# Turning the head order of a fused attention-and-MLP training step so that four V heads stay on the chip, with the middle of the kernel rewritten by columns

## The chip, the core and the metric

One core of one Trainium2 chip. The metric is the device time of the whole program in microseconds; it is given as the median of several runs. Engines: TensorE (PE), VectorE (DVE), ScalarE (ACT), GpSimd (POOL) and SyncE (SP), which here does little but issue DMA transfers. Sixteen DMA engines move the data between the memory (HBM) and the on-chip buffer.

## What is computed

A decode step of a pre-layernorm transformer block (4 sequences, one token each, 32 attention heads over a cache of 4096 positions, model width 512, a gated MLP of width 1792) and its gradients with respect to the input, the whole K and V caches and all weights.

```python
def _A_ref(x, k_cache, v_cache, wq, wo):      # x [4,1,512], caches [4,32,4096,128] bf16
    q = (x @ wq) split into 32 heads of 128
    scores = einsum("bhqd,bhkd->bhqk", q, k_cache) * 128 ** -0.5
    p = softmax(scores)
    o = einsum("bhqk,bhkd->bhqd", p, v_cache)
    return o.reshape(4, 1, 4096) @ wo
def _B_ref(x, w1, w3, w2):
    return (silu(x @ w1) * (x @ w3)) @ w2
h = x + _A_ref(layernorm(x), k_cache, v_cache, wq, wo)
out = h + _B_ref(layernorm(h), w1, w3, w2)
# returned: out, and the vector-Jacobian product with grad_out for
# x, k_cache, v_cache, wq, wo, w1, w3, w2
```

The caches make up nearly all of the traffic: 128 pairs of sequence and head ("heads" below, number s = 4 x head + sequence), each with 1 MiB of K and 1 MiB of V, are read, and gradients of the same sizes are written. V is read twice, once in the forward part and once in the backward part.

## The kernel before

**Memory.** One on-chip tile, `arena`, is cut by hand into 23 slots of 4160 bf16 columns (`Slot`, L125). A slot holds one head of K or V, one transposed K, one product P x K (`PK`), a page of weights or an outgoing gradient. Slots are handed out in the order of the program text from a queue of free ones; the hardware then waits until the last user of that slot is through. The program order is written out by hand (`manual_schedule`): each engine executes its instructions in the order of the text, and all large transfers, loads and stores alike, are issued on SP's queue in that order. A few small ones go through POOL's queue.

**Forward loop** (L650 to L712). 64 rounds of two heads. For each head K is transposed (a quarter by PE and ACT, three quarters by DVE), the scores are formed, softmax runs over a chain of small steps (`sm_max` to `sm_P`), P x K is formed on DVE (`PK_mul`), and PE accumulates V^T x [PK, P] (`M_mm`): a 128 x 128 matrix M, kept for the gradient of q, and the attention output as its last column. `M_end` adds the sums of P x K (`kP`), copies M out and returns the slots of PK and V. `kP_flush` (L490) turns the k sums of 32 heads into columns; `O_cols` (L501) collects attention outputs. Towards the end `weights` (L628) loads wo in four pages and w1 and w3 in two halves each into slots as they become free.

**The end of the forward part** (L714 to L746). The last three heads' M alternate with `attn_page` (L510): the attention output times wo, rows of 512 columns on PE, eight heads to a page, added to the rows of x (`hrows`) by DVE in three additions. `woT` transposes wo in place, two heads to a unit, sixteen units in all; of these two are done here.

**The middle** (L843 to L969). First `while free: load_V2()` queues V heads for the backward part into all slots that are free: heads 0 to 6. Then: layernorm of h by rows of 4 partitions, with the results transposed and spread; two wo units; the gate product, four units of `w13T` (transposing w1 and w3 in place, 16 units in all), the up product; the activation and its gradient on DVE; the twelve other w13 units; the down product for the gradient (`dn_ps`, L906), column by column, 112 matmuls. Then the slots of w1 and w3 come free, one becomes `reps`, and two more V heads are queued (7 and 8). The layernorm's backward gives dhT; `rep_ps` and `dO_columns` (L768) multiply it by the first transposed wo page; `grad_V(0)` and `grad_V(1)` write the first two outer products on DVE and store them. `V_T(0, ...)` transposes V of head 0 by pairs of words, four groups, each four PE transposes and one ACT copy: two groups ahead of dhT, two behind `dO_columns`.

**The backward loop** (L1457 on). For heads 0 to 31 one by one, then in pairs: `front(s)` (L1230) transposes V and forms dP on PE; `more_V` (L1416) writes V gradients ahead of that; after four heads the group's dS is formed and `grad_K` writes K gradients. Side work is spread over the heads by `side` (L1449): the rest of wo's transposes and dO (`rest_of_dO`, L1163, in heads O0 = 2 to S0 = 21), the gradient of q (`dq_work`, L1005), and all small gradients (from S1 = 35). The free slots of this part are chosen by age.

Of the kernel before, what the change touches and what calls it, by code (L numbers as in the profile page):

```python
# [15 lines left out]
G = 2  # L16
# [7 lines left out]
OLD = 9  # L24


@with_exitstack
def kernel(
# [38 lines left out]
    GW = 8  # L67
# [19 lines left out]
    def bh_of(s):  # L87
        return s % B, s // B

# [72 lines left out]
    rows_t = pers.tile([32 + B, D], FP32, name="rows_t")  # L162
    xr, xhat = rows_t[0:B, :], rows_t[32:32 + B, :]
    nc.gpsimd.dma_start(out=xr, in_=x2)
    gr_s = Slot("gr")
# [7 lines left out]
    Ks, Vs, KTs, PKs = {}, {}, {}, {}  # L173

    def load_K(s):
        if s < NH:
            Ks[s] = Slot("Kn")
            nc.sync.dma_start(out=Ks[s].heads(), in_=cache_head(A_k_cache, s))
# [3 lines left out]
    def load_V(s):  # L182
        if s < NH and s >= nvl["n"]:
            nvl["n"] = s + 1
            Vs[s] = Slot("Vn")
            nc.sync.dma_start(out=Vs[s].heads(), in_=cache_head(A_v_cache, s))
# [16 lines left out]
    sel_f = fcon.tile([P, H], FP32, name="sel_f")  # L203
# [37 lines left out]
    hrows = xr  # L241
    kPT = pers.tile([P, NH], FP32, name="kPT")
# [83 lines left out]

    def M_of(s):
        return Ms[s // MC].f(MC * (Dh + 1)).rearrange("p (n c) -> p n c", c=Dh + 1)[:, s % MC, :]
# [37 lines left out]
    def q_stationaries(gi):  # L366
        W = fw.tile([P, G, 4, 32], BF16, name="W", tag="W", bufs=1)
        for hl in range(G):
            s = gi * G + hl
# [69 lines left out]
    def sm_P(gi):  # L439
# [5 lines left out]
        for q in range(4):  # L445
            r_ = slice(32 * q, 32 * (q + 1))
            nc.scalar.copy(out=P_all[r_, gi * G:(gi + 1) * G, :].rearrange("p g (c jj) -> p g c jj", c=4),  # L447
                           in_=v[r_, 0:G, :, :, q])

    def PK_pairs(s):  # L450
        PKs[s] = Slot("PK")
        PK = PKs[s].t[:].rearrange("p (j c) -> p j c", c=PKW)
        nc.gpsimd.tensor_copy(out=PK[:, :, Dh:PKW], in_=P_all[:, s, :, None].to_broadcast([P, SJ, 2]))  # L453
# [20 lines left out]
    def M_end(s):  # L474
# [13 lines left out]
        Vs.pop(s).give()  # L488

    def kP_flush(s):  # L490
        ks = Slot("kP_sb")
        kP_sb = ks.f(4 * Dh).rearrange("p (c d) -> p c d", c=4)
        nc.scalar.copy(out=kP_sb, in_=hold["kP"][:])
        kt_ps = psM.tile([P, PKW], FP32, tag="M", name="kt_ps")
        for c in range(4):
            nc.tensor.matmul(kt_ps[:, 0:H], lhsT=kP_sb[:, c, :], rhs=sel_f[:], start=(c == 0), stop=(c == 3))
        nc.scalar.copy(out=kPT[:, s - 31:s + 1], in_=kt_ps[:, 0:H])
# [3 lines left out]
    def O_cols(s0, s1):  # L501
        nc.vector.tensor_copy(out=OT_f[:, s0:s1], in_=Ms[s0 // MC].f(MC * (Dh + 1)).rearrange("p (n c) -> p n c", c=Dh + 1)[
            :, s0 % MC:s0 % MC + s1 - s0, Dh])
        nc.vector.tensor_copy(out=OT_bf[:, s0:s1], in_=OT_f[:, s0:s1])
# [5 lines left out]
    def attn_page(pg):  # L510
        last = pg == H // 8 - 1
        if pg == 0 or last:
            hold["at"] = psT.tile([P, 512], FP32, tag="tps", name="al_ps") if last else psX.tile([P, 512], FP32, tag="x", name="at_ps")
        at_ps = hold["at"]
        for k in range(8):
            c = 0 if last else k % 2
            nc.tensor.matmul(at_ps[32 * c:32 * c + B, :], lhsT=OT_bf[:, (8 * pg + k) * B:(8 * pg + k + 1) * B],
                             rhs=wo_page(8 * pg)[:, k].rearrange("p c n -> p (c n)"),
                             start=(k == 0 if last else pg == 0 and k < 2), stop=(k == 7 if last else pg == H // 8 - 2 and k >= 6),
                             tile_position=(0, 32 * c))  # L520
        if pg >= H // 8 - 2:
            for c in range(1 if last else 2):
                nc.vector.tensor_tensor(out=hrows, in0=hrows, in1=at_ps[32 * c:32 * c + B, :], op=ALU.add)
# [67 lines left out]
    def w13T(n, eng=None):  # L591
        for k in range(n):
            w13T_unit(*tunits.popleft(), eng[k % len(eng)])

    def w13T_unit(nm, i, k, eng):
        n = min(4, FC - k)
        v = mid_w[nm][i].b(2 * F).rearrange("p (c f) -> p c f", c=2)[:, :, k * P:(k + n) * P]
        pt = psT.tile([P, 2, 4, P], BF16, tag="tps", name="pt_w13")
# [3 lines left out]
        evac_copy(v.rearrange("p c (n k) -> p c n k", k=P), pt[:, :, 0:n, :], eng)  # L602
# [16 lines left out]
    tunits = deque((nm, i, k) for nm in ("w1", "w3") for i in range(2) for k in range(0, FC, 4))  # L619

# [29 lines left out]
    for gi in range(NGI):  # L650
# [23 lines left out]
        if has1:  # L674
            M_end(m1)
            load_V(m1 + VQ)
            if m1 % 32 == 31:
                kP_flush(m1)
# [50 lines left out]
    attn_page(0)  # L729
# [3 lines left out]
    attn_page(1)  # L733
    woT(2, "sv")
# [3 lines left out]
    O_cols(NH - MC, NH)  # L738
    attn_page(2)
    attn_page(3)  # L740
    kP_flush(NH - 1)
    weights(NGI)
    assert not pending
    c1b.close()
# [14 lines left out]
    rstd_h = pers2.tile([B, 1], FP32, name="rstd_h")  # L759
    mv_h = pers2.tile([B, nc.vector.BN_AGGR_DIM], FP32, name="mv_h")  # L760
# [29 lines left out]
    V2s, VTs = {}, {}  # L790
# [43 lines left out]
    nv = {"next": 0}  # L834
# [8 lines left out]
    with ExitStack() as cm:  # L843
# [3 lines left out]
        psT = cm.enter_context(tc.tile_pool(name="psTm2", bufs=4, space=bass.MemoryType.PSUM))  # L847
        while free:
            load_V2()

        pt = psA.tile([P, DC, B], FP32, tag="rT", name="pt_hT")
        for c in range(DC):
            nc.tensor.transpose(pt[:, c, :], hrows[0:B, c * P:(c + 1) * P], ident_f[0:B, 0:B])
        stats = small.tile([B, 1, nc.vector.BN_STATS_DIM], FP32, tag="ln_stats", name="ln_stats")
        nc.vector.bn_stats(out=stats[:, 0, :], in_=hrows)
        mv = mv_h
        nc.vector.bn_aggr(out=mv[:], in_=stats[:])
        nc.vector.tensor_scalar(out=rstd_h[:], in0=mv[:, 1:2], scalar1=eps, scalar2=None, op0=ALU.add)
        nc.scalar.sqrt(rstd_h[:], rstd_h[:])
        nc.scalar.activation(out=warm[:], in_=warm[:], func=AF.Exp)  # L860
        woT(2, "s")
        rdiag = mid.tile([B, 2 * B], FP32, name="rdiag")
        nc.vector.tensor_scalar(out=rdiag[:, 0:B], in0=ident_f[0:B, 0:B], scalar1=mv[:, 0:1], scalar2=None, op0=ALU.mult)
        nc.vector.reciprocal(out=rstd_h[:], in_=rstd_h[:])
        nc.vector.tensor_scalar(out=rdiag[:, B:2 * B], in0=ident_f[0:B, 0:B], scalar1=rstd_h[:], scalar2=None, op0=ALU.mult)
        rb_ps = psA.tile([P, 2 * B], FP32, tag="rT", name="rb_ps")
        nc.tensor.matmul(rb_ps[:], lhsT=ones_f[0:B, :], rhs=rdiag[:], start=True, stop=True)
        rb = mid.tile([P, 2 * B], FP32, name="rb")
        nc.vector.tensor_copy(out=rb[:], in_=rb_ps[:])
        hhatT = mid.tile([P, DC, B], BF16, name="hhatT")  # L870
        hhatT_f = mid.tile([P, DC, B], FP32, name="hhatT_f")
        nc.vector.tensor_tensor(out=hhatT_f[:], in0=pt[:], in1=rb[:, None, 0:B].to_broadcast([P, DC, B]), op=ALU.subtract)
        nc.vector.tensor_tensor(out=hhatT[:], in0=hhatT_f[:], in1=rb[:, None, B:2 * B].to_broadcast([P, DC, B]), op=ALU.mult)
        nc.vector.tensor_tensor(out=hhatT_f[:], in0=hhatT_f[:], in1=rb[:, None, B:2 * B].to_broadcast([P, DC, B]), op=ALU.mult)
        w1, w3 = mid_w["w1"], mid_w["w3"]
        gu_ps = psC.tile([P, 2, FC, B], FP32, tag="cols", name="gu_ps")
        for wi, wt in enumerate((w1, w3)):
# [4 lines left out]
            if wi == 0:  # L882
                w13T(4, "sv")
# [663 lines left out]
```

## Time and profile before

| | |
|---|---|
| median of 3 runs | 1688.55 us (1687.66 to 1689.11) |
| span of the profiled execution | 1686.6 us |
| PE, DVE, ACT, POOL busy | 1260.6, 1233.9, 960.9, 379.6 us |
| DMA | 707.21 MB, mean 419 GB/s |
| chain that ended last, by engine | DMA 35%, DVE 7%, ACT 5%, PE 5% |
| mean granted TensorE clock | 0.855 |

The profile lists for one execution when each engine was busy and what it waited for. The chain of waits follows the work that ended last back to the start. The tables by stretches give for a window of time the busy microseconds of each engine with the number of instructions, the granted TensorE clock (1.00 is full speed), the mean busy share of the DMA engines and the rate. The lines for SP show when a transfer was issued, not when it landed; the time to landing is listed with the issues by line. Two rows of that list:

```profile
arena<-in_A_v_cache_dram SPq DMA_DIRECT2D x160, 1024.0 KB, 15.6
out_dram<-arena SPq DMA_DIRECT2D x72, 1024.0 KB, 19.8
```

The columns are what is moved, the issuing queue, the number of transfers, the size of each and the median time from issue to landing in microseconds: a transfer stands behind several others.

### The profile page before, as it was taken

How to read it: one execution, taken by the hardware profiler on the slowest of the kernel's cores; microseconds unless marked ns; L12 is line 12 of the kernel's file. 1: busy time of each engine (PE TensorE's matmuls, PEld its weight loads, DVE VectorE, ACT ScalarE, POOL GpSimd, SP SyncE). 2: the span in 40 equal slices, each digit the busy share in tenths (PEclk: the TensorE clock that was granted, in tenths of full speed). 3: DMA queues.
4: the chain of work that ended last, by engine and by line, in shares of the span. 5: the costliest groups of instructions: out<-in, count | busy, mean ns of one | idle time of the engine just before them, and what ended most of it. 6: DMA issues, size and time to landing. Idle time of an engine off the chain costs nothing.

```text
span 1686.6 us, 33967 instructions
## 1 busy us (share of the span) xinstructions
PE 1260.6 (75%) x14188; PEld 924.3 (55%) x14188; DVE 1233.9 (73%) x1198; ACT 960.9 (57%) x1492; POOL 379.6 (23%) x663
## 2 busy tenths in 40 slices
PE   5989888888888888878878666667766677776660
PEld 4777777677667766745555544544434444444440
DVE  5999899989998997667766476576565656555673
ACT  3455454445445454677666556666655676666650
POOL 1221222222232222234541131111120101011020
PEclk9999999999999999799899778777678676567775
DMA  9999999999999999999999999999999999999996
GB/s 400 424 424 424 425 423 425 424 424 421 418 423 411 424 411 397 398 410 426 425 426 428 429 429 429 431 430 429 429 430 430 429 429 431 430 429 431 430 429 259
DMA packets 80986, 707.21 MB, mean 419 GB/s; under 512 B 8748, under 2 KB 12984, under 8 KB 15296
## 3 DMA queue, kind: packets, MB, share of 16 engines
q1 hardware_dynamic: 80416, 704.94, 99.2%
q8 instruction: 112, 1.84, 0.4%
q14 instruction: 42, 0.34, 0.0%
q0 software_dynamic: 416, 0.10, 0.0%
HBM read 422.59 MB, written 282.34 MB: 418 GB/s over the span
## 4 chain that ended last, share of the span: by engine, by line
DMA 35%; DVE 7%; ACT 5%; PE 5%; issue 3%; DVEq 0%; SPq 0%; POOL 0%; ACTq 0%
DMA out_dram<-arena 34%; DVE arena L1400 7%; ACT arena L799 5%; PE pt_tps L798 1%; PE dq_ps L1007 1%; PE dP_ps L1245 1%; DMA arena<-in_A_v_cache_dram 1%; PE pt_wo L610 0%; DVEq L1542 0%; PE rep_ps L1186 0%; DVE dPr L1342 0%; ACT dPr L1221 0%; PE dOT_ps L773 0%; PE dPT_ps L1228 0%; PE c_ps L784 0%
## 5 line engine op out<-in xcount | busy, mean ns | idle before, releaser
L799 ACT COPY arena<-pt_tps 128x1024 bf16<-128x1024 bf16 x512 | 491.7, 1023 | 249.0 <-PE pt_tps L798 247.3
L798 PE MATMUL pt_tps<-ident_f,arena 128*128 128x128 f32 x2048 | 410.7, 356 | 202.9 <-DMA arena<-in_A_v_cache_dram 125.6
L798 PEld LDWEIGHTS pt_tps<-ident_f,arena 128*128 128x128 f32 x2048 | 304.1, 182 | 349.3 <-issue 191.6
L1400 DVE TENSOR_TENSOR arena<-arena 128x8192 bf16<-128x8192 bf16 x48 | 212.5, 4427 | 197.9 <-DMA out_dram<-arena 192.5
L457 DVE TENSOR_TENSOR arena<-arena 128x4096 bf16<-128x4096 bf16 x128 | 292.4, 2285 | 24.0 <-POOL arena L453 24.0
L472 PE MATMUL M_ps<-arena 128*128 128x130 bf16 x4096 | 286.9, 223 | 30.0 <-DMA arena<-in_A_v_cache_dram 29.2
L472 PEld LDWEIGHTS <-arena 128*128 128x128 bf16 x4096 | 254.6, 99 | 49.6 <-DMA arena<-in_A_v_cache_dram 42.5
L1400 DVE TENSOR_TENSOR arena<-dS,arena 128x8192 bf16<-128x8192 bf16 x48 | 212.3, 4424 | 67.6 <-DMA out_dram<-arena 67.6
L364 DVE STREAM_TRANSPOSE arena<-arena 128x512 f32<-128x512 f32 (+1 forms) x321 | 250.6, 797 | 0.0
L359 ACT COPY arena<-pt_tps 128x1024 bf16<-128x1024 bf16 x128 | 129.4, 1012 | 180.4 <-PE pt_tps L358 149.6
L1397 POOL COPY arena<-arena 128x128 bf16<-128x128 bf16 x48 | 43.7, 912 | 432.7 <-ACT arena L1374 200.0
L370 POOL TENSOR_TENSOR W<-qrep,wmask 128x128 bf16<-128x128 bf16 x128 | 120.8, 944 | 85.4 <-PE S_ps L390 70.6
L453 POOL COPY arena<-P_all 128x64 bf16<-128x64 bf16 x128 | 32.7, 256 | 412.5 <-ACT P_all L447 409.5
L1308 POOL COPY arena<-arena 64x4 bf16<-64x4 bf16 x96 | 68.8, 717 | 136.3 <-PE dP_ps L1328 108.6
L1328 PE MATMUL dP_ps<-arena 128*32 128x512 bf16 x768 | 84.4, 471 | 8.4 <-ACT arena L799 8.3
L813 DVE TENSOR_TENSOR arena<-dS,arena 128x4096 bf16<-128x4096 bf16 x32 | 73.1, 2291 | 21.8 <-DMA out_dram<-arena 21.5
L447 ACT COPY P_all<-pt_P 32x64 bf16<-32x64 bf16 x256 | 52.1, 203 | 54.1 <-PE pt_P L443 51.8
L358 PE MATMUL pt_tps<-ident_b,arena 128*128 128x128 bf16 x1024 | 80.8, 224 | 0.0
L482 PE MATMUL kP_ps<-arena,onesw 128*32 128x512 bf16 x1024 | 79.4, 387 | 0.0
L813 DVE TENSOR_TENSOR arena<-P,arena 128x4096 bf16<-128x4096 bf16 x29 | 66.3, 2291 | 17.7 <-DMA out_dram<-arena 17.5
L422 ACT ACTIVATE E<-S_ps,nm 128x256 f32<-128x256 f32 x64 | 30.4, 474 | 82.7 <-DVE nm L419 82.6
L991 PE MATMUL gps<-arena 4*128 4x512 bf16 x110 | 47.3, 452 | 39.0 <-ACT arena L985 39.0
(246 smaller groups left out, 1494.7 us busy)
## 6 DMA issues: line engine op xcount, KB each, us to landing
out_dram<-arena SPq DMA_DIRECT2D x96, 2048.0 KB, 27.4
arena<-in_A_v_cache_dram SPq DMA_DIRECT2D x160, 1024.0 KB, 15.6
arena<-in_A_k_cache_dram SPq DMA_DIRECT2D x128, 1024.0 KB, 15.4
arena<-in_A_v_cache_dram SPq DMA_DIRECT2D x48, 2048.0 KB, 31.7
out_dram<-arena SPq DMA_DIRECT2D x72, 1024.0 KB, 19.8
arena<-in_A_wq_dram SPq DMA_DIRECT2D x8, 1024.0 KB, 14.3
arena<-in_B_w_dram SPq DMA_DIRECT2D x8, 896.0 KB, 15.0
out_dram<-arena SPq DMA_DIRECT2D x6, 896.0 KB, 27.6
```

Of the source, the lines that this page charges most:

```text
L358: nc.tensor.transpose(pt[:, i, :], Kn[:, c * GW + i, :], ident_b[:])
L359: nc.scalar.copy(out=KT[:, c * GW:(c + 1) * GW, :], in_=pt[:])
L364: nc.vector.transpose(out=KT[:, c * w_:(c + n) * w_], in_=Kn[:, c * w_:(c + n) * w_])
L370: nc.gpsimd.tensor_tensor(out=W[:, hl], in0=qrep[:, :, s:s + 1].to_broadcast([P, 4, 32]), in1=wmask[:, hl, None, :].to_broadcast([P, 4, 32 ...
L457: nc.vector.tensor_tensor(out=PK[:, :, 0:Dh].rearrange("p j (r t) -> p j r t", t=2), in0=Ks[s].heads().rearrange("p j (r t) -> p j r t", t=2),
L472: nc.tensor.matmul(hold["M"][:], lhsT=Vn[:, j, :], rhs=PK[:, j, :], start=(j == 0), stop=(j == SJ - 1))
L482: nc.tensor.matmul(hold["kP"][32 * q:32 * (q + 1), :, :], lhsT=ones_window(w), rhs=PK[:, j0:j0 + 4, 0:Dh], start=(w == 0 and c == 0), stop ...
L798: nc.tensor.transpose(ptw[:, jj, :], w[:, 4 * g + jj, :], ident_f[:])
L799: nc.scalar.copy(out=v.rearrange("p (j d) -> p j d", d=Dh)[:, g * GW:(g + 1) * GW, :], in_=pt[:])
L813: nc.vector.tensor_tensor(out=dst.rearrange("p j (r t) -> p j r t", t=2), in0=col2[:, :, None, :].to_broadcast([P, SJ, Dh // 2, 2]), in1=r ...
L1328: nc.tensor.matmul(rows["acc"][32 * c:32 * (c + 1), :], lhsT=zt[t % B][:, k, ZP - m:ZP - m + 32], rhs=words_of(v, 2 * c + u, k), start=(pl ...
L1400: nc.vector.tensor_tensor(out=dst.rearrange("p (j r t) -> p j r t", r=Dh // 2, t=2), in0=col2[:, :, None, :].to_broadcast([P, 2 * SJ, Dh / ...
```

## The change

**Order and kept V.** The forward loop's step f works on column `col(f) = (f + 4) % 128`, so its last four steps are heads 0 to 3, with which the backward part begins. The loads, the query columns, the softmax results, the outputs and the k sums are placed by `col`. `M_end` doesn't return the V slots of these four; they become the first entries of `V2s`, and the backward part's loads of V start at head 4. The gradient of q runs over f in the same turned order.

**Attention by columns.** `attn_page` goes. `attn_x` starts a 128 x 16 accumulation in PSUM with the transposed x (four small loads of x, `xcols`, are new on POOL's queue at the start), and `attn_heads` adds four products of 4 columns for each head, heads 1 to 31 in order and head 0 among the last. One DVE copy gives h by columns (`hT_f`). No wo unit is left in this part.

**Layernorm by columns.** `col_sums` sums over partitions by a matmul with ones and over the four chunks by a DVE reduction; it runs twice, for the mean and for the variance. The row forms of h and of its normalised value, which are wanted much later, come from two more transposes at the end of `rest_of_dO`, for which S0 goes from 21 to 23. The last `kP_flush` moves into the layernorm.

**w1, w3 and the down product.** The first half of w1 is transposed into a slot of its own (`w1T`) in place of in place. One w13 unit runs in the layernorm, four and one wo unit between the gate and the up product, with the gate's activation chain. The first half's slot is then returned, and V is loaded into what is free. The other eleven units alternate with `dn_unit`s, parts of the down product that use what is transposed by then; the accumulation starts with a product of zeros.

**wo and V_T.** Three wo units stand where two groups of `V_T(0)` stood; all four groups of `V_T(0)` come after `grad_V(1)`.

```diff
+    def col(f):
+        return (f + KEEP) % NH
...
+    xcols = rows_t[64:64 + DC * B, 0:P]
+    for c in range(DC):
+        nc.gpsimd.dma_start(out=xcols[c * B:(c + 1) * B, :], in_=x2[:, c * P:(c + 1) * P])
...
-            nc.sync.dma_start(out=Vs[s].heads(), in_=cache_head(A_v_cache, s))
+            nc.sync.dma_start(out=Vs[s].heads(), in_=cache_head(A_v_cache, col(s)))
...
-        Vs.pop(s).give()
+        if s < NH - KEEP:
+            Vs.pop(s).give()
+        else:
+            kept[col(s)] = Vs.pop(s)
...
+    def kP_copy():
+        ks = Slot("kP_sb")
+        nc.scalar.copy(out=ks.f(4 * Dh).rearrange("p (c d) -> p c d", c=4), in_=hold["kP"][:])
+        return ks
+
+    def kP_flush(s, ks, kt_ps):
...
+        for f0, f1 in runs(s - 31, s + 1):
+            nc.scalar.copy(out=kPT[:, col(f0):col(f0) + f1 - f0], in_=kt_ps[:, f0 - (s - 31):f1 - (s - 31)])
         ks.give()
...
-    def attn_page(pg):
...
+    def attn_x():
+        hold["at"] = psX.tile([P, DC, B], FP32, tag="x", name="at_ps")
+        r_ = slice(64, 64 + DC * B)
+        nc.tensor.matmul(hold["at"].rearrange("p c b -> p (c b)"), lhsT=xcols, rhs=ident_f[r_, r_], start=True, stop=False)
+
+    def attn_heads(h0, h1, last=False):
+        for h in range(h0, h1):
+            for c in range(DC):
+                nc.tensor.matmul(hold["at"][:, c, :], lhsT=wo_page(h)[:, h % 8, c, :], rhs=OT_bf[:, h * B:(h + 1) * B],
+                                 start=False, stop=last and h == h1 - 1 and c == DC - 1)
...
-    attn_page(0)
+    O_cols(NH - MC, NH - KEEP)
+    attn_x()
+    attn_heads(1, 8)
     M_mm(NH - 2, 0, SJ)
     M_end(NH - 2)
     weights(NGI)
-    attn_page(1)
-    woT(2, "sv")
+    attn_heads(8, 16)
     M_mm(NH - 1, 0, SJ)
     M_end(NH - 1)
     weights(NGI)
-    O_cols(NH - MC, NH)
-    attn_page(2)
-    attn_page(3)
-    kP_flush(NH - 1)
-    weights(NGI)
+    O_cols(NH - KEEP, NH)
+    attn_heads(16, 24)
+    attn_heads(0, 1)
+    attn_heads(24, H, True)
...
+    nc.vector.tensor_copy(out=hT_f[:], in_=hold["at"][:])
+    ks_last = kP_copy()
...
-    V2s, VTs = {}, {}
+    V2s, VTs = dict(kept), {}
...
-    nv = {"next": 0}
+    nv = {"next": KEEP}
...
+        w1T = Slot("w1T")
+        mid_t.update(w1=[w1T, mid_w["w1"][1]], w3=mid_w["w3"])
         while free:
             load_V2()
...
+        def w13T(n, eng):
+            for k in range(n):
+                u_ = tunits.popleft()
+                w13T_unit(*u_, eng[k % len(eng)])
+                turned.append(u_)
...
+        def col_sums(src, name):
+            ps = psA.tile([P, DC, B], FP32, tag="rT", name="cs_ps")
+            nc.tensor.matmul(ps.rearrange("p c b -> p (c b)"), lhsT=ones_f[:], rhs=src.rearrange("p c b -> p (c b)"),
+                             start=True, stop=True)
+            s_ = mid.tile([P, B], FP32, name=name)
+            nc.vector.tensor_reduce(out=s_[:], in_=ps.rearrange("p c b -> p b c"), axis=AX.X, op=ALU.add)
+            return s_
...
+        hsum = col_sums(hT_f, "hsum")
+        nc.vector.scalar_tensor_tensor(out=hc[:], in0=hsum[:, None, :].to_broadcast([P, DC, B]), scalar=-1.0 / D,
+                                       in1=hT_f[:], op0=ALU.mult, op1=ALU.add)
+        nc.vector.tensor_tensor(out=sq[:], in0=hc[:], in1=hc[:], op=ALU.mult)
...
+        w13T(1, "s")
+        rb = col_sums(sq, "rb")
...
+        kP_flush(NH - 1, ks_last, psA.tile([P, PKW], FP32, tag="rT", name="kt_ps"))
...
             if wi == 0:
-                w13T(4, "sv")
...
+                nc.scalar.activation(out=sigT[:], in_=gu_ps[:, 0], func=AF.Exp, scale=-1.0)
+                w13T(2, "ss")
...
+                woT(1, "s")
+                w13T(2, "vs")
+                w1[0].give()
+                while free:
+                    load_V2()
...
-        w13T(len(tunits), "sssvsvsvsvvs")
...
+        nc.tensor.matmul(dn_ps.rearrange("p c b -> p (c b)"), lhsT=ident_b[:], rhs=zeros[:], start=True, stop=False)
...
+        def dn_unit(nm, i, k):
+            lt = d_gateT_bf if nm == "w1" else d_upT_bf
+            for jj in (2 * i, 2 * i + 1):
+                for fc in range(k, min(k + 4, FC)):
+                    nc.tensor.matmul(dn_ps[:, jj, :], lhsT=w13_view(mid_t[nm], jj)[:, fc * P:(fc + 1) * P], rhs=lt[:, fc, :],
+                                     start=False, stop=n_dn["n"] == 2 * DC * FC - 1)
+                    n_dn["n"] += 1
+
+        engs = deque("svsvsvvsvsv")
+        while turned:
+            if tunits:
+                w13T(1, engs.popleft())
+            if len(tunits) < 9:
+                for _ in range(2 if tunits else len(turned)):
+                    if len(turned) > (2 if tunits else 0):
+                        dn_unit(*turned.popleft())
...
-        V_T(0, psT, range(2))
+        woT(3, "s")
...
-        V_T(0, psT, range(2, SJ // GW))
+        V_T(0, psT)
...
-        O0, S0, S1, L, LP = 2, 21, 35, 5, 3
+        O0, S0, S1, L, LP = 2, 23, 35, 5, 3
```

## The prediction, made before the changed kernel had run

> **What bounds the kernel now.** I read the page's slices first, then the middle in rows of 4 us, then SP's issues, then PE, ACT and DVE there in order of time.
>
> ```profile
> DMA  9999999999999999999999999999999999999996
> GB/s 400 424 424 424 425 423 425 424 424 421 418 423 411 424 411 397 398 410 426 425 426 428 429 429 429 431 430 429 429 430 430 429 429 431 430 429 431 430 429 259
> HBM read 422.59 MB, written 282.34 MB: 418 GB/s over the span
> ```
>
> The DMA engines are full in every slice but the last; no compute engine is above 75% over the span. So time is bytes over rate, plus the places where the rate drops: the slices of 397 and 398 (the turn from forward to backward) and the end. A head of K or V is 1 MiB: at 427 GB/s 2.455 us.
>
> The turn, in the table by stretches (PE, PEld, DVE, ACT, POOL busy, then TensorE clock, DMA share, GB/s):
>
> ```profile
> 680.00:684.00 4.00, 4.00 (x91) 4.00 (x88) 1.12 (x2) 2.38 (x5) 0.00 (x0) 0.60 1.01 423
> 684.00:688.00 4.00, 4.00 (x43) 4.00 (x42) 2.48 (x11) 3.32 (x6) 0.00 (x0) 0.55 1.01 422
> 688.00:692.00 4.00, 3.89 (x103) 3.77 (x101) 2.38 (x4) 3.19 (x4) 0.00 (x0) 1.00 1.02 430
> 692.00:696.00 4.00, 3.77 (x76) 3.40 (x73) 1.42 (x8) 1.50 (x3) 0.22 (x1) 0.81 0.95 348
> 704.00:708.00 4.00, 3.71 (x17) 2.95 (x16) 3.07 (x2) 3.14 (x4) 2.25 (x2) 0.50 0.75 313
> 708.00:712.00 4.00, 2.76 (x21) 1.46 (x20) 3.63 (x3) 2.67 (x4) 0.43 (x3) 0.99 0.88 369
> 720.00:724.00 4.00, 3.03 (x25) 2.11 (x20) 1.67 (x5) 2.91 (x4) 2.24 (x7) 1.00 0.94 293
> ```
>
> PE is full at half clock until 688 while DMA still has work; DMA runs short only from 692 on. Against 427 GB/s the rows from 692 to 712 lose 2.6 us, those from 712 to 724 another 1.7.
>
> SP's issues (start, time to the last of the group, line, transfers):
>
> ```profile
> 651.71 11.10 SPq L586 DMA_DIRECT2D arena<-in_A_wo_dram  x4
> 662.91 6.51 SPq L580 DMA_DIRECT2D arena<-in_B_w_dram  x4
> 669.51 24.92 SPq L840 DMA_DIRECT2D arena<-in_A_v_cache_dram  x9
> 699.11 17.89 SPq L824 DMA_DIRECT2D out_dram<-arena  x7
> ```
>
> Behind the weights SP queues seven V heads (17.2 us of DMA) that cover the MLP; the last two of the nine wait for the down product and go out at 693.2. The first store of a V gradient follows at 699.1. Issue by issue, the four w1/w3 halves land at 675.1, 677.3, 679.5 and 681.5 (the last: issued 667.25, 14.3 to landing).
>
> Engines in order of time, PE first:
>
> ```profile
> 682.03 1.68 PE L880 MATMUL gu_ps<-hhatT,arena 128*128 128x4 bf16 x56
> 683.64 7.04 PE L601 MATMUL pt_w<-ident_b,arena 128*128 128x128 bf16 x84
> 694.19 1.71 PE L798 MATMUL pt_tps<-ident_f,arena 128*128 128x128 f32 x8
> 702.45 1.04 PE L1245 MATMUL dP_ps<-arena,zd 128*32 128x512 bf16 x8 [1.28 <-POOL zd L1211]
> ```
>
> ```profile
> 698.95 1.93 ACT L799 COPY arena<-pt_tps 128x1024 bf16<-128x1024 bf16 x2 [0.77 <-PE pt_tps L798]
> ```
>
> ```profile
> 703.71 2.31 DVE L813 TENSOR_TENSOR arena<-arena 128x4096 bf16<-128x4096 bf16 x1 [2.00 <-POOL zd L1211]
> ```
>
> The third store's outer product (703.71) starts just after front(0)'s dP product (702.45 + 1.04): counting slots by hand, it takes the slot that front(0) returns. From there DVE makes one store per 2.31 us, about what DMA takes, so **the time of dP in front(0) sets when DMA is full again**.
>
> **Part by part.**
>
> **Bytes.** Four V heads are not read again: 4 x 2.455 = **-9.8 us** of DMA. The turned column order adds no instruction in the loops.
>
> **Start.** Four small loads of x stand on POOL's queue ahead of the load of grad_out and the identity. Two such issues took 0.67 and 0.55 us, so POOL is some 2.4 us later; its identity (2.76) feeds the q product by way of 9.56, which then waits until 13.53 for wq. 3.1 us of cover: 0; without it 2.4.
>
> **Slots.** By the same count w1, w3 and wo go to slots as early as now (the last w3 half takes one freed after head 125, 664.5, before its issue at 667.25). But the four kept heads and w1T occupy five slots, so behind the weights only three V heads are queued in place of seven: one once head 127 is through (671), one after the flushed k sums (676), one after w1's first half is transposed (681). Heads 0 to 8 are in SBUF when the backward loop starts, as now.
>
> **Attention, layernorm.** 32 products of 512 columns (1.03 three times, 1.89) and three row adds (2.07) become 128 of 4 columns at 0.0275 (56 in 1.54) = 3.5, one of 0.4 and one copy of 0.17; two wo units (1.07) leave the stretch before M of head 127. I get the last attention product at 672.7 in place of 674.8. Layernorm: two sums of 0.4, two reduces of 0.19, four small DVE steps, the root 0.2: gate could start at 675.7 in place of 678.5. But w1's second half lands at 677.3. So gate 677.4 to 678.9, and 2.8 us of saving shrink to 1.1. Were that wrong by 1.7 us, the landing would still hide it.
>
> **Between gate and up.** Five w13 units and a wo unit: 44 transposes less the 8 done in the layernorm = 36, at 0.067 (16 in 1.07) 2.4 us, held a little by ACT (three evictions of 1.01): 681.4. Then w3 must have landed: 681.5. **Up starts at 681.6, 0.4 before now**, and ends at 683.2. This is the floor that nothing in the change moves.
>
> **Transposes and down.** 76 transposes remain (84 now) and 112 down products (0.0252 each: 28 per 0.705). A transpose costs 0.067 at full clock and 0.093 in the row 684 to 688 (43 in 4.00). That row bounds it; I take the middle, 0.080: 6.1 + 2.8 + 0.15 for the last eviction = down ends at 692.3, now 693.5: **-1.2** (bounds -2.2 and -0.2). The gate's DVE chain before up, and the mixing, hide only what DVE and ACT had idle; PE is full.
>
> **Down to the first stores.** Three wo units (24 transposes, 1.9) stand where eight fp32 transposes stood (1.71): -1.0 is left; first store 698.1. All four groups of V_T(0) now come behind dO_columns (ends 697.4): first group 0.75 (8 took 1.07 to 1.97), then four evictions of 0.965 on ACT: 702.0, where two ended at 700.9. Queued behind them on ACT are the dO rows and dOw, then POOL's windows, then dP. So **dP, the third store and all after: +1.1**; third store issued at 707.15, now 706.04.
>
> **Rest.** Two more row transposes and copies (0.6 each) at heads 20 to 22, the turned dq order, one more copy in the flush: in a stretch where DMA is full at 424 to 430 and PE at most 0.9 busy: 0; uncovered some 2.
>
> **Sum.** DMA's gaps in the new turn, with 0.9 us from an issue to its first packet (third store now: issued 706.04, packets from 706.9). The queue empties at 694.5 - 9.8 = 684.7, say 685; next load 692.0 + 0.9: **7.9**. Two loads to 697.8, first store 699.0: **1.2**. Two stores to 703.9, third 708.05: **4.1**. Together 13.2. So -9.8 + 13.2 - 2.6 (today's gaps there) = +0.8. The loss of 1.7 at 712 to 724 may stay or go; the rows after it carry the same mix at 424 and more, so I let it go: -1.7 (bounds 0, -1.7). Last, the slowest DMA engine: in the rows after 1670 of this trace one engine alone works off the end, share 0.12 and 0.03; after the third store its share of a transfer lands up to 1.2 us after the others', and a gap in which all stand still lets it catch up: -1.1 (bounds 0, -1.2). Total **-2.0 us**: 1684.6 in place of 1686.6 in the profiled execution, which lies 1.95 under the median of the runs; so **1686.5** against 1688.55. Bounds: the transposes 1.0 either way, wo units with V_T's first group 0.6, and the two last terms at nothing 2.8: 1684.9 to 1691.
>
> By the Trainium skill (TensorE: Matmul & The Clock Gate, Part 1) the half clock is PE's default and some 3.4 us of sustained work release it. Here PE was busy 4.00 of 4.00 us in two rows at 0.60 and 0.55, so the trace does not bear it out at this place; by the rule the transposes would cost 0.067, and the sum be 1685.5.
>
> **Rivals.**
>
> **The handover closes** (0.38). Only the first gap is certain: its start is the bytes', its end the down product's. If the third store came by 703.5, gaps two and three vanish: -9.8 + 7.9 - 2.6 - 1.7 - 1.1 = -7.3: 1681. For: ACT is idle 2.5 us before 693.8 and PE transposes need no ACT until then; a full clock alone gives 2 of the 3.7 us needed. Against: that slot wait.
>
> **Fronts at half clock** (0.18), the slower side. dP of front(0) to front(1) took 6.9 us at the 0.50 of 704 to 708, 5.2 later at 1.00. If the gaps shift the half clock past 708, dP(0) is 1.3 later still and three fronts cost 1.7 more each: the first K store leaves at 734 instead of 727, past the 733 to which the earlier transfers keep DMA busy. -2.0 + 1.3 + 1.7 + 2.8 (no catch-up, dips stay) = +3.8, 1692. It decides from two half-clock stretches after 708.
>
> **The forecast** (0.44): the middle is held by the weights' landing, and the bytes saved come back as idle DMA.
>
> **Numbers.** 0.2% is 3.4 us, about what can be told from no change. Forecast: 0.08 faster, 0.34 within, 0.02 slower; closing rival all faster; slow rival 0.13 slower, 0.05 within. So 0.46, 0.39, 0.15. Range 1679 (2 below the closing rival, whose later terms are as uncertain as the sum's) to 1692.5; the forecast's own 1684.9 to 1691.
>
> **What would show it.** HBM read lower by 4.2 MB. Up at 681 to 682. A row near 0 GB/s between 685 and 693, shorter ones at 698 and 704 to 708. First store near 698, third near 707. Wrong if up starts before 680.5, if the third store leaves before 704, or if the stretch after 735 runs below 424.

## The result and the profile after

The changed kernel takes **1698.21 us** (median of 4 runs, 1697.58 to 1699.59) against 1688.82 us for the kernel before in the same session: a ratio of 1.0058, 95% interval 1.0043 to 1.0072. It is slower by some 9.8 us by the ratio; 1686.5 had been forecast, and 1698.2 lies outside the range. The profiled execution's span is 1695.8 us in place of 1686.6.

The page of the kernel after, its DMA slices, rates and volume:

```profile
DMA  9999999999999999799999999999999999999995
GB/s 397 418 419 418 420 418 419 419 419 418 414 414 408 419 399 397 306 407 425 426 425 427 428 429 429 428 430 431 429 430 430 429 429 429 429 430 430 429 428 255
HBM read 418.40 MB, written 282.34 MB: 413 GB/s over the span
```

Two things differ from before. Slice 17 falls to 306: that is the turn, with the gaps that were forecast. And slices 2 to 10, deep in the forward loop, read 418 to 420 where they read 421 to 425, with DMA full in both. Nothing was forecast there.

The table by stretches (columns as before: PE, PEld, DVE, ACT, POOL busy, TensorE clock, DMA share, GB/s), three stretches of the kernel before:

```profile
50.00:200.00 150.00, 132.48 (x2213) 107.26 (x2214) 137.74 (x186) 81.15 (x174) 33.54 (x90) 1.00 1.01 424
200.00:400.00 200.00, 170.72 (x2832) 141.36 (x2831) 185.21 (x244) 98.37 (x223) 53.51 (x120) 0.98 1.01 423
1100.00:1600.00 500.00, 348.01 (x1973) 217.35 (x1973) 306.51 (x162) 323.65 (x412) 68.87 (x100) 0.70 1.01 430
```

and of the kernel after:

```profile
50.00:200.00 150.00, 132.64 (x2189) 108.23 (x2187) 135.70 (x181) 79.57 (x168) 33.60 (x90) 0.98 1.01 419
200.00:400.00 200.00, 167.03 (x2803) 137.45 (x2803) 183.70 (x242) 98.06 (x223) 52.70 (x116) 1.00 1.01 419
1100.00:1600.00 500.00, 347.87 (x1980) 218.88 (x1979) 304.99 (x156) 325.00 (x412) 69.61 (x101) 0.70 1.01 429
```

The share stays 1.01: the DMA engines never rest, they move 1% less per unit of time, from the first heads on. So no wait is to blame. The loss is all there when the loop ends: the last K load (step 127) is issued at 641.00 us in place of 632.82 (+8.18), w1 at 671.04 in place of 662.91 (+8.13). The backward part runs at its old rate (429 and 430).

The trace also has the time of each DMA packet. In the forward loop a packet is the 8192 bytes that one partition gets of a head. The table is counted from the traces' packet records:

```
8192-byte packets, 100 to 600 us    mean ns   309 or less   310-313   314-317   318-320
before                               311.9        94%          2%        1%        1%
after                                316.0        15%         54%       11%       19%
8192-byte packets, 760 to 900 us
before                               310.0        96%          1%        1%        1%
after                                310.4        94%          1%        1%        1%
```

316.0 / 311.9 over 633 us is 8.3 us, the delay seen. In the backward part, where loads and stores alternate, there is no difference.

The turn of the kernel after, shifted by 8.1 us against the forecast's clock. The table by stretches:

```profile
692.00:696.00 4.00, 4.00 (x113) 4.00 (x110) 1.94 (x5) 3.00 (x5) 0.00 (x0) 1.00 0.76 307
696.00:700.00 4.00, 3.56 (x93) 3.40 (x90) 2.04 (x4) 2.22 (x3) 0.00 (x0) 1.00 0.60 215
700.00:704.00 4.00, 3.45 (x63) 3.12 (x63) 1.89 (x11) 2.71 (x5) 0.22 (x1) 1.00 0.82 320
704.00:708.00 4.00, 3.29 (x53) 2.97 (x50) 3.96 (x4) 3.44 (x6) 0.24 (x1) 1.00 0.27 111
708.00:712.00 4.00, 1.35 (x14) 0.42 (x14) 0.85 (x2) 2.01 (x4) 2.55 (x13) 0.86 1.04 426
712.00:716.00 4.00, 3.45 (x20) 2.61 (x18) 3.85 (x2) 2.99 (x4) 3.84 (x4) 0.72 0.19 80
```

SP's issues there (start, time to the last of the group, line, transfers):

```profile
671.04 6.48 SPq L594 DMA_DIRECT2D arena<-in_B_w_dram  x4
679.66 19.49 SPq L853 DMA_DIRECT2D arena<-in_A_v_cache_dram  x5
706.24 8.58 SPq L837 DMA_DIRECT2D out_dram<-arena  x3
```

Five V heads where nine were, a row at 0.19 before the third store (issued 714.49), one at 0.27 before the first (706.24). Less 8.13 these stores stand at 706.4 and 698.1: forecast were 707.15 and 698.1. The turn went about as worked out; the time was lost in a part that the prediction had left as it was.

**The theory.** The change moves `sel_f` (128 bytes a partition) to `const` and adds `hT_f` (64) to `pers`; both pools lie ahead of `arena`:

```diff
-    sel_f = fcon.tile([P, H], FP32, name="sel_f")
+    sel_f = const.tile([P, H], FP32, name="sel_f")
...
+    hT_f = pers.tile([P, DC, B], FP32, name="hT_f")
```

In the compiled program `arena` starts at byte 30336 of each partition before and at 30528 after. (The traces list no addresses; what the runs below show is the effect of each shift.) 30336 is 237 x 128; 30528 is an odd multiple of 64. A slot is 8320 bytes, 65 x 128, so the whole arena keeps that remainder: every load of the forward loop starts off a multiple of 128. The picture behind the theory is that a packet then touches 65 lines of 128 bytes in place of 64. By that picture 309 ns would become 313.8, an estimate; measured are 310 to 320 and a mean 4.1 ns higher. So the size is about right, but what a packet does inside is not shown by any run. The rivals: the four small x loads, which run on POOL's queue at the start, and the turned order of the heads in HBM.

### The profile page after: what moved, and what is told of

It is laid out like the page before. It is cut to its first block, busy times and chain, and to the rows that moved or that the text cites. A ratio compares the mean times of both kernels' runs of the same rounds, so it can differ in the third digit from the quotient of the medians.

```text
span 1695.8 us, 34176 instructions
## 1 busy us (share of the span) xinstructions
PE 1262.4 (74%) x14293; PEld 929.6 (55%) x14293; DVE 1230.6 (73%) x1195; ACT 963.1 (57%) x1496; POOL 383.4 (23%) x668
## 4 chain that ended last, share of the span: by engine, by line
DMA 35%; DVE 7%; ACT 6%; PE 5%; issue 2%; POOL 1%; DVEq 0%; SPq 0%; ACTq 0%; POOLq 0%
DMA out_dram<-arena 33%; DVE arena L1442 7%; ACT arena L812 5%; DMA arena<-in_A_v_cache_dram 2%; PE pt_tps L811 2%; PE dq_ps L1048 1%; PE dP_ps L1287 1%; POOL zd L1253 1%; POOL P L1258 0%; PE pt_wo L621 0%; DVEq L1584 0%; PE rep_ps L1228 0%; DVE dPr L1384 0%; ACT dPr L1263 0%; PE dOT_ps L786 0%
## 5 line engine op out<-in xcount | busy, mean ns | idle before, releaser
L483 PEld LDWEIGHTS <-arena 128*128 128x128 bf16 x4096 | 254.6, 100 | 74.2 <-DMA arena<-in_A_v_cache_dram 68.5
L369 PEld LDWEIGHTS <-arena 128*128 128x128 bf16 x1024 | 61.7, 99 | 25.7 <-issue 25.6
```

Of the source, the lines that this page charges most:

```text
L369: nc.tensor.transpose(pt[:, i, :], Kn[:, c * GW + i, :], ident_b[:])
L483: nc.tensor.matmul(hold["M"][:], lhsT=Vn[:, j, :], rhs=PK[:, j, :], start=(j == 0), stop=(j == SJ - 1))
```

## The experiments

All ratios are to the kernel before, run on the same chip in the same session, with 95% intervals.

**Is it the address alone?** Two unused tiles in the kernel before, of the sizes that the change adds:

```diff
+    const.tile([P, H], FP32, name="pad_c")
+    pers.tile([P, DC, B], FP32, name="pad_p")
```

> The kernel before with two unused tiles (128 and 64 bytes per partition) ahead of the slots, so that arena begins at byte 30528 of a partition, as in the changed kernel, in place of 30336; nothing else. Address theory (a slot that begins at an odd multiple of 64 bytes costs each 8 KB packet of a load one more 64-byte beat): most forward packets take 312 ns and more, 419 GB/s in place of 424, the loop ends some 8 us later, 1697 us. Small-load theory and order theory: 1688.5 us, packets at 309 ns.

Measured: 1698.55 us, ratio 1.0058 (1.0043 to 1.0073). 192 idle bytes give the whole loss; the last K load is issued at 640.90, and the packets' mean is 315.7.

**The x loads alone**, in the kernel before:

```diff
-    rows_t = pers.tile([32 + B, D], FP32, name="rows_t")
+    rows_t = pers.tile([P, D], FP32, name="rows_t")
+    xcols = rows_t[64:64 + DC * B, 0:P]
+    for c in range(DC):
+        nc.gpsimd.dma_start(out=xcols[c * B:(c + 1) * B, :], in_=x2[:, c * P:(c + 1) * P])
```

> The kernel before with the four small loads of x on POOL's queue at the start (unused), nothing else; arena stays at byte 30336. Small-load theory (they leave the sixteen DMA engines in another phase to each other, which lasts as long as they are full): forward rate 419 GB/s, 1697 us. Address theory and order theory: 1688.5 us, 424 GB/s.

Measured: 1688.72 us, 1.0001 (0.9992 to 1.0011). They cost nothing, as the prediction had it.

**The turned order alone**: the heads of the forward loads moved on by four in the kernel before, q left in its old order.

```diff
-            nc.sync.dma_start(out=Ks[s].heads(), in_=cache_head(A_k_cache, s))
+            nc.sync.dma_start(out=Ks[s].heads(), in_=cache_head(A_k_cache, (s + 4) % NH))
...
-            nc.sync.dma_start(out=Vs[s].heads(), in_=cache_head(A_v_cache, s))
+            nc.sync.dma_start(out=Vs[s].heads(), in_=cache_head(A_v_cache, (s + 4) % NH))
```

> The kernel before, whose forward loop reads K and V of head s+4 in place of s (the addresses alone are turned: q and the caches are then paired wrongly, which changes values and no work). Order theory (the memory answers the turned order more slowly): 419 GB/s, 1697 us. Address theory and small-load theory: 1688.5 us, 424 GB/s.

Measured: 1688.56 us, 1.0001 (0.9991 to 1.001). The turned order costs nothing.

**The changed kernel without the x loads**; x comes by PE transposes and a product with the identity, `arena` stays at 30528.

```diff
-    for c in range(DC):
-        nc.gpsimd.dma_start(out=xcols[c * B:(c + 1) * B, :], in_=x2[:, c * P:(c + 1) * P])
...
+        rows_to_T(ps0, hT_f[:], xr, B, DC)
...
-        nc.tensor.matmul(hold["at"].rearrange("p c b -> p (c b)"), lhsT=xcols, rhs=ident_f[r_, r_], start=True, stop=False)
+        nc.tensor.matmul(hold["at"].rearrange("p c b -> p (c b)"), lhsT=ident_f[:], rhs=hT_f.rearrange("p c b -> p (c b)"),
+                         start=True, stop=False)
```

> The changed kernel without the four small loads: the columns of x come from four transposes of its rows on PE at the start, and enter the attention sum through a product with the identity. arena stays at byte 30528. Small-load theory: forward back to 424 GB/s, 1690 us. Address theory and order theory: 419 GB/s, 1698 us.

Measured: 1697.76 us, 1.0053 (1.0037 to 1.007). The loss stays; both rivals fall.

**The changed kernel with its slots back on 128**: one unused tile of 64 bytes, `arena` at 30592 = 239 x 128.

```diff
     hT_f = pers.tile([P, DC, B], FP32, name="hT_f")
+    pers.tile([P, DC, B], FP32, name="pad_p")
```

> The changed kernel with one unused tile of 64 bytes ahead of the slots: arena begins at byte 30592 in place of 30528, an even multiple of 64 again, like 30336 before. Address theory: the forward loop is back at 424 GB/s and the time falls by some 9.5 us to 1688. What is left is the change as it was forecast: the idle-DMA account (bytes saved come back as gaps) puts it at 1686.5 to 1689. If the saved bytes counted in full, 1679; if the middle itself were worse, over 1692.

Measured: 1688.85 us (11 runs, 1686.65 to 1690.43), 0.9999 (0.9991 to 1.0008). The padding wins back the loss, and no more: **without its accident of layout the change is worth nothing that can be measured.** The same stretches in this run, and the slices' rates:

```profile
50.00:200.00 150.00, 131.59 (x2210) 106.79 (x2207) 137.01 (x185) 80.94 (x173) 33.84 (x90) 1.00 1.01 424
200.00:400.00 200.00, 170.91 (x2833) 141.53 (x2832) 185.29 (x244) 98.45 (x223) 53.75 (x120) 0.98 1.01 424
...
GB/s 400 424 425 424 424 423 425 424 424 421 418 424 408 424 413 396 298 409 426 424 426 427 430 428 429 428 428 431 426 427 429 430 430 430 428 428 429 429 429 272
```

The forward loop is at 424 again and the last K load is issued at 632.85, as before. What is left is slice 17 at 298.

**Which shift matters.** 64 bytes alone ahead of `arena` in the kernel before (30400):

```diff
+    pers.tile([P, DC, B], FP32, name="pad_p")
```

> The kernel before with an unused tile of 64 bytes alone ahead of the slots: arena at 30400, an odd multiple of 64. Address theory in this form (only the odd 64 bytes count, not the distance moved): 1697 to 1699 us, forward 419 GB/s. If what counts is the 192 bytes, or which tiles share a stretch of memory: 1688.5 us.

Measured: 1698.33 us, 1.0057 (1.0042 to 1.0072). In `a_aligned` the same tile repairs what it breaks here, so it is the remainder and not the tile.

32 bytes (30368):

```diff
+    pers.tile([P, 8], FP32, name="pad_p")
```

> The kernel before with an unused tile of 32 bytes a partition ahead of the arena, which then starts at 32 past a multiple of 128. If a packet pays whenever its 8192 bytes straddle one more block of 64 or 128 bytes, it loses as much as the shift by 64: 1698.5 us (1697 to 1700). If only the half of a 128-byte block counts, or the unit is 32 bytes, it is 1688.6. If several partial beats are paid, it is slower still.

Measured: 1698.45 us, 1.006 (1.0044 to 1.0075); packets' mean 316.1, 13% at 309 or less. A shift by 32 costs what one by 64 costs. That fits lines of 128 bytes, of which a shifted packet touches one more, however much of it is used. It doesn't fit units of 64 bytes, as `b_pad`'s expectation has them: a start moved by 64 would cut 8192 bytes into no more of those.

**Half of the slots**: a gap of 64 bytes behind slot 11 of the kernel before.

```diff
+    def at(i):
+        return i * SLOT + (32 if i >= ODD else 0)
...
-            self.t = arena[:, self.i * SLOT:(self.i + 1) * SLOT]
+            self.t = arena[:, at(self.i):at(self.i) + SLOT]
```

> The kernel before with a gap of 64 bytes in the middle of the arena: slots 0 to 11 start at multiples of 128 bytes as before, slots 12 to 22 at odd multiples of 64. If each load packet pays for its own slot's start, 11 of 23 slots pay: about 48% of the 10.0 us that the two runs with all slots shifted lost, 1693.3 us (1692 to 1695), and about half of the packets that take 309 ns before take 312 or 319. If the loss came from anything else that moves with the start of the arena (its total size, the tiles ahead of it), it is none (1688.6) or all of it (1698.5).

Measured: 1692.85 us, 1.0026 (1.0016 to 1.0036): 4.4 us over the kernel before, against 9.8 with all slots shifted. In the same packet table 60% take 309 ns or less and 38% from 310 to 320, mean 313.7. Each packet pays for its own slot's start. `arena` itself starts at 30336 here, so nothing ahead of it can be the cause.

**Are the saved bytes idle DMA?** The four kept heads read once more into their own slots, in the aligned kernel, behind the last V load between gate and up: 9.8 us of transfers put back.

```diff
                 while free:
                     load_V2()
+                for s in range(KEEP):
+                    nc.sync.dma_start(out=V2s[s].heads(), in_=cache_head(A_v_cache, s))
```

> The aligned changed kernel that also reads the four kept V heads a second time, into their own slots, behind the last V load between gate and up: the bytes of the kernel before, the rest of the change. Idle-DMA account: the four transfers (9.8 us of DMA) fall into the gap of some 8 us before the down product's end and the one of 4 us ahead of the third store, and the time moves by no more than +1.5 us. If bytes bound this stretch: +9.8 us.

Measured: 1688.96 us, 1.0007 (0.9998 to 1.0016). Over the aligned kernel that is 0.1 us by the medians and some 1.3 by the ratios, of 9.8 put back. The table by stretches of the aligned kernel, rows from 676 to 712:

```profile
676.00:680.00 4.00, 4.00 (x73) 4.00 (x74) 1.05 (x7) 2.85 (x7) 0.00 (x0) 0.50 1.02 392
680.00:684.00 4.00, 4.00 (x66) 4.00 (x64) 1.75 (x7) 3.56 (x4) 0.00 (x0) 0.50 0.95 337
684.00:688.00 4.00, 4.00 (x73) 4.00 (x71) 1.25 (x4) 2.16 (x4) 0.00 (x0) 0.50 0.70 285
688.00:692.00 4.00, 4.00 (x111) 4.00 (x110) 1.81 (x4) 1.76 (x2) 0.00 (x0) 0.99 0.26 47
692.00:696.00 4.00, 3.35 (x70) 3.01 (x67) 2.31 (x10) 2.53 (x4) 0.00 (x0) 1.00 0.96 352
696.00:700.00 4.00, 3.60 (x66) 3.35 (x64) 3.27 (x6) 3.44 (x5) 0.22 (x1) 1.00 0.34 139
700.00:704.00 4.00, 1.13 (x11) 0.79 (x9) 2.04 (x2) 3.22 (x6) 1.73 (x7) 1.00 0.94 393
704.00:708.00 4.00, 3.62 (x24) 2.52 (x24) 3.04 (x2) 2.51 (x3) 3.78 (x8) 0.64 0.32 131
708.00:712.00 4.00, 3.29 (x22) 1.80 (x20) 4.00 (x3) 2.42 (x3) 3.90 (x3) 0.93 1.01 422
```

and with the heads read again, from 680 (the row before reads 396):

```profile
680.00:684.00 4.00, 4.00 (x79) 4.00 (x78) 2.02 (x8) 3.40 (x5) 0.00 (x0) 0.72 0.91 341
684.00:688.00 4.00, 4.00 (x111) 4.00 (x108) 1.93 (x5) 2.92 (x5) 0.00 (x0) 1.00 0.98 401
688.00:692.00 4.00, 3.01 (x82) 2.94 (x79) 1.71 (x3) 1.48 (x3) 0.00 (x0) 1.00 1.01 420
692.00:696.00 4.00, 3.27 (x62) 2.85 (x60) 1.84 (x9) 2.71 (x4) 0.22 (x1) 1.00 1.01 422
696.00:700.00 4.00, 3.60 (x62) 3.28 (x59) 3.78 (x5) 3.44 (x5) 0.00 (x0) 1.00 1.02 428
700.00:704.00 4.00, 1.05 (x14) 0.52 (x14) 1.40 (x2) 2.57 (x5) 2.22 (x10) 0.84 0.96 350
704.00:708.00 4.00, 3.71 (x24) 2.62 (x16) 2.91 (x2) 2.44 (x3) 3.15 (x7) 0.50 0.87 369
708.00:712.00 4.00, 3.51 (x22) 1.89 (x20) 3.81 (x2) 2.42 (x4) 0.24 (x1) 0.80 0.97 408
```

The holes are filled: against 427 GB/s the nine rows lose 2.9 us in place of 12.6. The end hardly moves: third store 707.05 against 707.33. (The two executions differ in the clock too, 0.72 against 0.50 from 680 to 684, so it is the medians and ratios that say how little time the bytes cost.) The bytes were saved where DMA then has nothing to do.

**Can dP(0) come earlier?** V_T(0)'s four groups moved to the end of the forward part, two ahead of `O_cols` and two behind the first run of attention products, in the aligned kernel:

```diff
+    early_T(range(2))
     O_cols(NH - MC, NH - KEEP)
     attn_x()
     attn_heads(1, 8)
+    early_T(range(2, SJ // GW))
...
-        V_T(0, psT)
```

> The aligned changed kernel with all four groups of V_T(0) in the forward part's end, two after M of head step 125 is issued and two after the first attention products, where ACT is idle: V of head 0 has been there since the forward loop. Theory that dP of front(0) sets when DMA is full again: dP some 2.5 to 3.5 us earlier, the third store 2.9 earlier, 1684 to 1686.5. Rival (the first K store, paced by the later fronts, or the landing of w3 sets it): within 1 us of the aligned kernel. If the two us that PE gets more ahead of the gate product delay up: no gain or a loss of up to 1.

Measured: 1688.11 us, 1.0001 (0.9992 to 1.001). dP of front(0) starts at 704.16 and not earlier (704.09 in the aligned kernel): the expectation was missed. The timeline of POOL (start, length, line, operation; in brackets idle time before and who ended it) in that run:

```profile
701.70 1.69 POOL L814 CAST dOT_f<-dOT_bf 128x32 f32<-128x32 bf16 x1 [4.10 <-PE c_ps L812]
703.32 0.40 POOL L1246 MEMSET zd<- 128x64 bf16 x4
703.67 0.91 POOL L1260 COPY zd<-dOw 64x2 bf16<-64x2 bf16 x4
```

and of DVE:

```profile
701.02 2.29 DVE L834 TENSOR_TENSOR arena<-arena 128x4096 bf16<-128x4096 bf16 x1
703.23 0.18 DVE L813 COPY c_rep<-c_ps 128x32 f32<-128x32 f32 x1
```

The dO words are ready at 702.1, 1.4 us earlier than in the aligned kernel; but POOL is in a cast until 703.4. So the cast was put behind the copies of zd in a last run:

```diff
+        if s0 == 0:
+            late.append((s0, s1))
+        else:
+            late_cast(s0, s1)
...
         for s in range(3, 6):
             P_pairs(s)
+        late_cast(*late.pop())
```

> The changed kernel with the padding that puts the slots back on multiples of 128 bytes, V_T(0)'s four groups at the end of the forward part, and the copy of the dO columns on POOL behind front(0)'s windows in place of ahead of them. In the run with the early groups alone dO words were there at 702.1 us, but POOL filled zd only from 703.7, behind that copy (1.7 us) and the memset. Then the products of dP in front(0) start at 702.5 to 702.9 in place of 704.2, and the third store goes out at 706.0 to 706.4 in place of 707.6. If the time of that store sets the end one for one, the run is 1.3 us below the one with the early groups: 1686.8 us; if DMA's gaps are merely moved, it stays at 1688.1 to 1688.8. Either way it stays within 0.2% of the kernel before.

Measured: 1687.70 us (1686.35 to 1691.11), 0.9997 (0.9988 to 1.0006): no faster than the kernel before by what can be told, and dP(0) at 704.25, again not earlier. POOL and DVE in that run:

```profile
702.81 1.86 POOL L1268 COPY zd<-dOw 64x2 bf16<-64x2 bf16 x4 [4.28 <-ACT dOw L1262]
704.73 0.58 POOL L1273 COPY P<-P_all 128x64 bf16<-128x64 bf16 x3
705.25 0.21 POOL L809 CAST dOT_f<-dOT_bf 128x32 f32<-128x32 bf16 x1
```

```profile
701.60 2.29 DVE L842 TENSOR_TENSOR arena<-arena 128x4096 bf16<-128x4096 bf16 x1
703.81 0.18 DVE L818 COPY c_rep<-c_ps 128x32 f32<-128x32 f32 x1
```

The cast, 1.69 us above, takes 0.21 here; now the zd copies take 1.86 in place of 0.91. In both runs it is the POOL instruction that falls under DVE's outer product that is long, and it ends with that product (701.02 + 2.29 = 703.31; 701.60 + 2.29 = 703.89; the long copy alone ends at 703.94). The Trainium skill (SBUF — State Buffer, "Who interferes with whom") has this as a lock: a two-input DVE instruction with both inputs in SBUF keeps a GpSimd instruction that reads SBUF and is issued after it waiting until it ends. The trace agrees. By this reading POOL, and with it dP(0), waits for the end of `grad_V(1)`'s product.

That product itself came later in both runs. In the aligned kernel it starts at 699.65, and up at 683.04; in the run with the early groups up starts at 684.53:

```profile
699.65 2.29 DVE L827 TENSOR_TENSOR arena<-arena 128x4096 bf16<-128x4096 bf16 x1
```

```profile
684.53 1.68 PE L918 MATMUL gu_ps<-hhatT,arena 128*128 128x4 bf16 x56
```

dP(0) starts 2.2 us behind the product's end in the aligned kernel, 0.9 and 0.4 in these two runs; but the product ends 1.4 and 1.9 later. Sixteen transposes moved ahead of the gate take PE some 2.2 us there, and gate and up start 1.5 (2.0 in the last run) later, as the expectation had feared. So what was won behind the product was lost ahead of it. How much of the delay is the moved groups' alone isn't shown: the last K load, too, went out 1.1 and 0.8 us later in these two executions. A version with that product behind the windows was not run.

## Why the prediction was wrong

**The step that failed** is the sentence under "Bytes": "The turned column order adds no instruction in the loops." That is true, and the forward loop was costed at nothing on the strength of it. No term looked at where the added tiles put the slots: 192 bytes cost 8.2 us by the end of the loop. Nor did the list of what would prove it wrong have the forward loop's rate; "the stretch after 735 below 424" watched the wrong side (427 GB/s from 735 to 1100 us, 429 from there to 1600).

The other steps can be judged on the aligned kernel, which has the change without the shift:

- **Bytes, -9.8**: right. HBM read fell by 4.19 MB.
- **Start, 0**: right, by the run with the x loads alone.
- **Slots**: right in number, three V heads and two more, five in all. But the two did not wait for the down product's end (694.0): they went out at 690.20 and 692.02, each as soon as the products that read its slot were done (690.1 and 691.9).
- **Attention and gate**: attention ends at 673.6 (forecast 672.7), gate starts at 677.7 (677.4 to 678.9): right.
- **Between gate and up**: wrong by 1.4. Up starts at 683.0, not 681.6. The four units and one between are 36 transposes as forecast, but took 4.0 us (679.24 to 683.25), not 2.4: the clock is 0.50 in three rows, 676 to 688, with PE busy 4.00 of 4.00 in each. The term was worked out at a full-clock price, and "the floor that nothing in the change moves" was the landing; the clock was the later of the two. In the shifted kernel it happened to come to 682.9 as well (691.04 less 8.13). How long the half clock lasts differs from one execution to the next: by the traces' clock records it is 13.7 us on end here, 6.8 in the kernels before and after and in the run with the heads read again.

```profile
677.72 1.66 PE L911 MATMUL gu_ps<-hhatT,arena 128*128 128x4 bf16 x56
679.24 1.87 PE L613 MATMUL pt_w<-ident_b,arena 128*128 128x128 bf16 x16
681.76 1.49 PE L613 MATMUL pt_w<-ident_b,arena 128*128 128x128 bf16 x12
683.04 1.68 PE L911 MATMUL gu_ps<-hhatT,arena 128*128 128x4 bf16 x56
```

- **Transposes and down**: 10.9 us from up to the end of the down product, 10.7 forecast: right, 1.7 late with up's start (694.0 against 692.3).
- **First store** 699.43 (698.1), **third store** 707.33 (707.15): the third is right, +1.3 against before where +1.1 was said. The down product's delay of 1.7 shrank on the way: 1.3 at the first store, 0.5 at dP(0) (704.09; forecast 702.45 + 1.1), 0.2 at the third store.
- **The gaps**: nine rows from 676 to 712 lose 12.6 us against 427 GB/s (13.2 forecast). The sum is right, the parts are not: the first four rows, which hold the gap before the down product's end, lose 6.1 (7.9 forecast), the later ones 6.5 (5.3). That these errors cancel is luck. The run that reads the heads again shows that the gaps are the saved time come back.
- **The dips at 712 to 724, -1.7**: didn't go. Those three rows lose 1.55 us in the aligned kernel.
- **The slowest engine, -1.1**: didn't come. From the issue of the last store to the last packet it is 26.5 us both before and in the aligned kernel.

-9.8 + 12.6 - 2.6 = +0.2 us is the sum without the two last terms; the spans differ by +0.7, the ratio is 0.9999. So **the forecast's mechanism, "the bytes saved come back as idle DMA", held**. The gain of 2.0 that it forecast came out of the two last terms alone, -2.8, which were only argued, and neither came. The 8 to 10 us that made the kernel slower came from none of the rivals. The slower rival, half clock in the fronts, had no part: rows after 708 of the kernel after are at 0.72 and above.

One loss of about 1 us is not placed: the span grew by 9.2 us, the forward loop by 8.2. It is no more than two executions of one kernel can differ (1687.66 to 1689.11 for the kernel before).

## What to carry to other kernels

Where a stretch is bound by loads, a tile of a few bytes put ahead of a large hand-cut buffer is part of the change's cost: work out the buffer's new start and keep it, and the pitch of its pieces, at the remainder by 128 that it had. When all stretches of one kind run a per cent slower with DMA full, look at the time of single packets before looking for a wait. And saving bytes is worth time only where DMA would have had other bytes to move: next to a gap where DMA waits for a result, the saved transfer widens the gap. Last, one trace can mislead by 1 us: from the gate to the first store it is 21.7 us in the trace of the aligned kernel and 20.7 in that with the heads read again, with a longer and a shorter half clock. A step of that size is judged by many runs.

## What the runs showed of the hardware

Packets of loads of 8192 bytes a partition take 309 ns (94% of them) when they start on a multiple of 128 bytes of the partition; 32 or 64 bytes off it some 54% take 310 to 313 and 18 to 19% 318 to 320: 424 against 419 GB/s. It shows only in the stretch that does nothing but load; with loads and stores mixed the packets take 309 (16384-byte ones 611) in either layout, and no run tells why. The Trainium skill (DMA: Bandwidth & Descriptors, "How a descriptor splits into AXI transactions") has a price for a start that isn't a multiple of 256. Here the starts of neighbouring slots are 32 x 256 + 128 bytes apart, so one of every two is off such a multiple; yet in the kernel before 94% of the forward loop's packets take 309: on the side of the on-chip buffer the unit is 128 at most, not 256.

TensorE was granted half its clock for 12 us on end, 676 to 688 in the aligned kernel, with PE busy 4.00 of 4.00 us in each row.
